# A planned attention-and-experts kernel: deeper buffers, and half of the output blocks turned by DMA instead of TensorE

## The chip, the cores and the metric

The kernel runs on one core of one Trainium2 chip. The metric is device time in microseconds, the median of several runs. The engines are named as the profile names them: PE (TensorE, with PEld for its weight loads), DVE (VectorE), ACT (ScalarE), POOL (GpSimd) and SP (SyncE, which here only issues DMAs). A name with a q behind it (SPq, POOLq) is that engine's instruction sequencer.

## What is computed

The reference is an attention with a learned feature map, followed by a mixture of experts whose routing weights come from eight rounds of row and column scaling. Cut to what matters:

```python
# q, k, v: (8 batches, 8 heads, 576, 64); w_phi: (64, 128)
def phi(x):
    proj = x @ w_phi
    proj = proj - max(abs(proj), axis=-1)
    return concat([exp(proj), exp(-proj)], axis=-1)      # 256 features
q_p, k_p = phi(q), phi(k)
kv = k_p.T @ v;  z = sum(k_p, over the 576 positions)
attn = (q_p @ kv) / (q_p @ z + 1e-6)
x = attn, heads side by side                              # (4608, 512)
P = exp(x @ w_gate - max);  8 times: P /= row sums; P /= column sums; P *= N / E
out = sum over 8 experts e of P[:, e] * (relu(x @ w1[e]) @ w2[e])   # w1: 512x1024
```

## The kernel before

**Tiles.** A batch has 8 heads, taken two at a time: four *pairs* per batch, 32 pairs in all, numbered 0 to 31. A *half* is two pairs and is what one load brings. Of the 576 positions 512 are the main part; the 64 that remain of a batch (the *rest*) are treated for all its heads together. The result x is kept turned, with features on the partitions, in `xT` (four blocks of 128 features by 4608 positions), because every later matmul wants it so.

**Steps.** `pair_a` makes the scores of a pair: matmuls of the turned keys and queries (`qkT`) with `wphi`, the maxima on VectorE (line 459), the exponentials on ScalarE (line 463), and the scaling of v on POOL (line 592). `queries` is its second half. `pair_b` sums keys times values into `kv` and multiplies with the query features (lines 666 and 671); VectorE scales these (lines 678 to 691) into a block `xb`. `pair_c` turns `xb` into `xT`: four TensorE transposes (line 705) into a PSUM bank and one VectorE copy (line 708). `rest_a` and `rest_c` do the same for a batch's rest; the rest's v is scaled by POOL (lines 525 and 529) into `vrd`. `gate` makes a batch's routing logits `L`. `up0` and `down0` are the two layers of expert 0 for one group of 512 positions; they need no routing weights, so they fill TensorE while attention and routing run. Experts 1 to 7 follow with a seven-product matrix scheme (line 1079).

**Loads.** For batches 0 and 1 SP loads q and k in f32 into the accumulators' memory (line 389), and TensorE turns them (line 544). From batch 2 on POOL loads and casts them to bf16 in `qk` (line 395), and a DMA issued by SP turns a half of them into `qkT` (line 412); rests likewise (line 487, `rT`). v comes by SP (line 403). Expert 0's weights come in eight pieces by POOL (lines 371 and 376), those of an expert e from 1 on in two loads of 1 MB (line 361), for expert 1 once `xT` of batch 5 is complete.

**Order.** Nothing is run as written. Each instruction is an `Op` with an estimated duration, the values it reads and writes, and the buffers it takes from a `Ring` of two, three or more. `Plan.schedule` places at each moment the operation that can start first, and by number where several can; the numbers follow the string `order`, one letter for each step (a, q, r, b, c, g, u and d for `up0` and `down0`). What comes out is one fixed row of instructions for each engine, and each engine then works through its row in order. The key `late` marks the point at which the attention's buffers are given back; accumulators 5 to 8 and the later scratch memory `s_p` lie in their place.

Of the kernel before, what the change touches and what calls it, by code (L numbers as in the profile page):

```python
# [9 lines left out]
FP32 = mybir.dt.float32  # L10
# [218 lines left out]
def kernel(  # L229
# [11 lines left out]
    nc = tc.nc  # L241
# [35 lines left out]
    identf = a_in.tile([128, 128], FP32, name="identf")  # L277
    wgate_f = a_in.tile([128, NP, E], FP32, name="wgate_f")
    wphi_f = a_in.tile([128, DF], FP32, name="wphi_f")
# [33 lines left out]

    ring(wp, [128, 4, FF], BF16, "w1", 2)
    ring(wp, [128, 8, DD], BF16, "w2", 2)
    ring(hp, [128, 4, 512], BF16, "hT", 4)
# [3 lines left out]
    ring(a_in, [128, 3 * NP, D], FP32, "v_r", 2)  # L320
    ring(a_t, [128, NP, 128], BF16, "rT", 2)
    ring(a_t, [128, 2, 8, 128], BF16, "qkT", 2)
    ring(a_t, [128, 2, 2, D1], BF16, "kv", 2)
# [3 lines left out]
    ring(a_s, [128, 2, 8], FP32, "m", 2)  # L327
    ring(a_s, [128, 12], FP32, "r", 2)
    ring(a_s, [128, 6], FP32, "rec", 3)
    ring(a_s, [128, NP, 128], BF16, "xb_r", 2)  # L330
    for x in range(2):
        ring(a_t, [128, NP, DF], BF16, f"kr{x}", 2)
        ring(a_t, [128, NP, 128], BF16, f"qr{x}", 2)
        ring(a_t, [128, 8, DF], BF16, f"k{x}", 2)
        ring(a_t, [128, 2, 4, 128], BF16, f"q{x}", 2)
        ring(a_t, [128, 8, D1], BF16, f"v{x}", 2)
        ring(a_s, [128, NP], FP32, f"em_r{x}", 2)
        ring(a_s, [128, 8], FP32, f"em{x}", 2)
    ring("s_p", [128, 1024], BF16, "T", 9)
# [26 lines left out]
    def load_w0(i, r):  # L366

        w1, w2 = W[0]
        n = i % 4
        if i < 4:  # L370
            dma("POOL", 1 << 19, 250, lambda: nc.gpsimd.dma_start(
                out=w1()[:, :, n * 256:(n + 1) * 256],
                in_=moe_w1[0].rearrange("(c p) f -> p c f", p=128)
                [:, :, n * 256:(n + 1) * 256]), r, [(w1, n)])
        else:
            dma("POOL", 1 << 19, 280, lambda: nc.gpsimd.dma_start(
                out=w2()[:, 2 * n:2 * n + 2, :],
                in_=moe_w2[0].rearrange("(c p) f -> p c f", p=128)
                [:, 2 * n:2 * n + 2]), r, [(w2, n)])

    def load_qk(b, hh, nh, t, r=()):

        o = hh % 4
        keys = [o // 2] if nh == 2 else [0, 1]
        if b < 2:
            g = t["f"]
            for x, src in ((1, k), (0, q)):
                i = 2 * x + o // 2
                dma("SP", nh << 17, 320, lambda x=x, src=src, i=i: nc.sync.dma_start(  # L389
                    out=acc[g][:, i:i + nh // 2].rearrange("p a (h c) -> p (a h) c", h=2),  # L390
                    in_=src[b, hh:hh + nh, 0:SM].rearrange("h (p j) d -> p h (j d)", j=NJ)),
                    r, [("acc", g, 2 * x + n) for n in keys])
            return
        for x, src in ((1, k), (0, q)):
            dma("POOL", nh << 17, 230, lambda x=x, src=src: nc.gpsimd.dma_start(
                out=t["qk"]()[:, x, o:o + nh],
                in_=src[b, hh:hh + nh, 0:SM].rearrange("h (p j) d -> p h (j d)", j=NJ)),
                r, [(t["qk"], x, i) for i in keys])

    def load_v(b, hh, nh, t, r=()):  # L400
        o = hh % 4
        keys = [o // 2] if nh == 2 else [0, 1]
        dma("SP", nh << 17, 320, lambda: nc.sync.dma_start(
            out=t["v"]()[:, o:o + nh],
            in_=v[b, hh:hh + nh, 0:SM].rearrange("h (p j) d -> p h (j d)", j=NJ)),
            r, [(t["v"], i) for i in keys])
# [24 lines left out]
    def load_rests(b0, nb, r=()):  # L431
        t = {"v": new("v_r"), "b0": b0}
        if b0 >= 2:
            t["qk"] = new("qk_r")
        for h in range(2):
            rows = slice(h * 64, h * 64 + 64)

            def part(src, h=h):
                return src.rearrange("b (r h) s d -> h s (b r) d", h=2)[
                    h, SM:S, NP * b0:NP * (b0 + nb)]  # L440

            for x, src in ((1, k), (0, q)):
# [6 lines left out]
                dma("POOL", nb << 16, 90, lambda rows=rows, x=x, src=src, part=part:  # L449
                    nc.gpsimd.dma_start(out=t["qk"]()[rows, 0:NP * nb, x, :], in_=part(src)),  # L450
                    r, [(t["qk"], h, x)])
# [17 lines left out]
    def rest_a(b, t):  # L469
# [6 lines left out]
        if b < 2:  # L476
            ptr = new("P1")
            for pr in range(NP):
                pe(128, lambda pr=pr: nc.tensor.transpose(
                    ptr()[:, pr * 128:pr * 128 + 128],  # L480
                    acc[0][:, b, pr * 128:pr * 128 + 128], identf),
                    [("acc", 0, b, h, x) for h in range(2) for x in range(2)] + ["identf"],
                    [ptr, ("acc", 0, b)])
            dve(512, lambda: nc.vector.tensor_copy(
# [35 lines left out]
        for x, s in ((0, -1.0), (1, 1.0)):  # L520
            em = r["em"][x]
            exp(10, lambda em=em: em(), lambda: m()[:, :, 1], s, mk, [em])
            for h in range(2):
                rows = slice(h * 64, h * 64 + 64)
                pool(256, lambda rows=rows, h=h, x=x, em=em: nc.gpsimd.tensor_tensor(
                    out=vrd[b % 2][x][rows, :, h, 0:D], in0=t["v"]()[rows, bi:bi + NP],
                    in1=em()[rows, :, None].to_broadcast([64, NP, D]), op=ALU.mult),
                    [(t["v"], h), em], [("vrd", b % 2, x, h)])
                pool(4, lambda rows=rows, h=h, x=x, em=em: nc.gpsimd.tensor_copy(
                    out=vrd[b % 2][x][rows, :, h, D], in_=em()[rows]),  # L530
# [3 lines left out]
    def pair_a(b, pr, t):  # L534
# [3 lines left out]
        if b < 2:  # L538
            g = t["f"]
            for x in (1, 0):  # L540
                ptr = new("P1")
                i = 2 * x + h0 // 2
                for c in range(4):
                    pe(128, lambda c=c, i=i, ptr=ptr: nc.tensor.transpose(
                        ptr()[:, c * 128:(c + 1) * 128], acc[g][:, i, c * 128:c * 128 + 128],
                        identf), [("acc", g, i), "identf"], [ptr])
                if x:
# [55 lines left out]
        def queries():  # L603

            mq = scores(0, 1)
            for p0 in range(0, 2, 1):
                pt = new("P1")
                for par in range(1):
                    pe(512, lambda par=par, p0=p0, pt=pt: mm(
                        pt()[:, 512 * par:512 * par + 512], wphi2[:, p0 + par, :], qkT(0, 0, 4),  # L610
                        True, True), [(t["T"], 0, h0 // 2), "wphi2"], [pt])
                for y, sg in ((0, 1.0), (1, -1.0)):
# [9 lines left out]
    def pair_b(b, pr, s, r):  # L622
# [29 lines left out]
        def outs(h):  # L652
# [8 lines left out]
            def feats(x):  # L661
# [3 lines left out]
                for j in range(4):  # L665
                    pe(65, lambda j=j: nc.tensor.matmul(  # L666
                        num()[:, j, :], lhsT=s["T"][x]()[:, j % 2, 2 * h + j // 2, :],
                        rhs=kv()[:, x, h, :], start=x == 0 and j == 0, stop=x == 1,
                        skip_group_check=True), keys, [pn])
                if h == 0:  # L670
# [30 lines left out]
    def pair_c(b, pr, xb):  # L701
        if b < 8:
            pxt = new("P1")
# [107 lines left out]
    dma("ACT", 1 << 15, 100, lambda: nc.scalar.dma_start(out=wphi_f[0:64, :], in_=w_phi),  # L811
        w=["wphi_f0"])
    dma("ACT", 1 << 15, 100, lambda: nc.scalar.dma_start(out=wphi_f[64:128, :], in_=w_phi),
        w=["wphi_f1"])
    load_v(0, 0, 2, halves[0, 0])
# [16 lines left out]
    dve(128, lambda: nc.vector.memset(colw, float(E) / float(N)), w=["colw"])  # L832
    dma("SP", 1 << 14, 50, lambda: nc.sync.dma_start(
        out=wgate_f, in_=moe_w_gate.rearrange("(c p) e -> p c e", p=128)), w=["wgate_f"])
    act(32, lambda: nc.scalar.copy(out=wgate, in_=wgate_f), ["wgate_f"], ["wgate"])

    rs, st, qs = {}, {}, {}
# [28 lines left out]
    def stage_g(b):  # L866
# [7 lines left out]
    order = (  # L874
        "raqaqabbccqaqbbaqrbaccuqrbgaqaquabcucbqccaruqbcabqdaqbacbugdqdaqubdccuubauacuqqd"
        "drcbagubqbdaqrduabccauqccubqdcbcuadgqgrbuadqbacaudqbqaddcbaurqcuqbcaadubqauabdqd"
        "gbuccdaqdqbdcbqcuuacbgcqcbcg"
    )
# [406 lines left out]
    for e in range(1, E):  # L1285
        w1, w2 = load_w(e, [("xT", 5, 3)])
        if e == 1:
# [49 lines left out]
```

## Time and profile before

| | |
|---|---|
| median of 3 runs | 1040.92 us (1040.34 to 1041.95) |
| the profiled execution's own time | 1041.77 us |
| its span, first to last instruction | 1040.0 us |
| granted TensorE clock | 0.999 |
| busy share of the span: PE, DVE, ACT, POOL | 98%, 79%, 68%, 44% |
| DMA | 93.94 MB, mean 90 GB/s |

A PE that is busy is not a PE at its peak: matmuls overlap and their ends are modelled, so that only longer idle times show. A DMA share is the mean over 16 engines, and goes over 1 where packets of two queues lie in an engine at the same time.

### The profile page before, as it was taken

The page shows a single profiled execution, that of the slowest core. Times are in us where ns is not written, and L with a number is a line of the kernel's source. Part 1 is how long each engine was busy: PE and PEld are TensorE (multiplying, and loading weights), DVE is VectorE, ACT ScalarE, POOL GpSimd, SP SyncE. Part 2 cuts the span into 40 slices and gives each one's busy share as a digit, 9 for nine tenths or more (in the row PEclk, how much of TensorE's full clock was granted, in tenths as well). Part 3 has the DMA queues.
Part 4 walks back from the last instruction along what each step waited for, and adds up shares of the span by engine and source line. Part 5 has one row for each costly group of instructions (what it writes and reads, how often), then busy time and mean ns, then how long its engine had stood idle before and what let it go on. Part 6 is the DMA issues. An engine that isn't in the chain of part 4 may idle for free.

```text
span 1040.0 us, 24497 instructions
## 1 busy us (share of the span) xinstructions
PE 1014.6 (98%) x9473; PEld 842.0 (81%) x9512; DVE 821.6 (79%) x1626; ACT 711.6 (68%) x1570; POOL 462.2 (44%) x532
## 2 busy tenths in 40 slices
PE   6889999999999999999999999999999999999998
PEld 4556666654788888888888888888888888888886
DVE  6999999988777787778876877788777877787675
ACT  7999999945976666666666665666666656666663
POOL 3886775500234444444434444344444444434442
PEclk9999999999999999999999999999999999999999
DMA  8999979534411161113311441134111611114333
GB/s 240 161 186 144 156 122 173 88 142 112 82 43 51 41 125 50 42 42 83 82 42 42 92 89 45 42 70 99 48 42 48 127 42 42 42 46 128 114 131 122
DMA packets 105237, 93.94 MB, mean 90 GB/s; under 512 B 45344, under 2 KB 80288, under 8 KB 105120
## 3 DMA queue, kind: packets, MB, share of 16 engines
q1 hardware_dynamic: 71840, 68.45, 24.2%
q0 software_dynamic: 33120, 23.86, 16.5%
q8 instruction: 74, 1.21, 0.5%
q14 instruction: 43, 0.35, 0.1%
q10 hardware_dynamic: 160, 0.07, 0.0%
HBM read 94.98 MB, written 14.16 MB: 105 GB/s over the span
## 4 chain that ended last, share of the span: by engine, by line
PE 89%; ACT 3%; DVE 3%; DMA 3%; issue 1%; SPq 0%; DVEq 0%; ACTq 0%
PE P L1079 71%; PE P L467 16%; ACT acc L1241 2%; DMA acc<-in_q_dram 1%; DMA qkT<-qk 1%; PE P L666 1%; DVE m L459 1%; ACT V L1231 1%; PE P L705 1%; ACT U L1107 0%; SPq L389 0%; DVE xb L686 0%; ACT hT L1116 0%; DVE P L678 0%; PE P L671 0%
## 5 line engine op out<-in xcount | busy, mean ns | idle before, releaser
L1234 POOL TENSOR_TENSOR acc<-acc,V 128x512 f32<-128x512 f32 x248 | 317.4, 1287 | 441.0 <-ACT V L1231 437.5
L1111 DVE CUSTOM_DVE_ANT_0 hT<-P,U 128x512 bf16<-128x512 f32 x378 | 255.4, 688 | 129.9 <-ACT U L1107 81.4
L1107 ACT COPY U<-P 128x512 f32<-128x512 f32 x378 | 217.4, 590 | 125.4 <-PE P L1079 120.9
L1231 ACT ACTIVATE V<-P 128x256 f32<-128x256 f32 x496 | 205.8, 476 | 134.7 <-PE P L1079 123.5
L1079 PEld LDWEIGHTS <-w 128*128 128x128 bf16 x2016 | 197.2, 98 | 24.3 <-issue 1.2
L1079 PEld LDWEIGHTS <-S 128*128 128x128 bf16 x1984 | 194.1, 98 | 23.1 <-issue 0.6
L1219 DVE SCALAR_TENSOR_TENSOR acc<-P,acc 128x256 f32<-128x256 f32 x372 | 159.3, 478 | 54.4 <-PE P L1079 51.9
L1079 PEld LDWEIGHTS <-T 128*128 128x128 bf16 x1512 | 147.9, 98 | 18.5 <-issue 1.4
L1079 PEld LDWEIGHTS <-hT 128*128 128x128 bf16 x1488 | 145.4, 98 | 18.2 <-DVE hT L1111 1.1
L1079 PE MATMUL P<-X,w 128*128 128x256 bf16 x1008 | 154.8, 273 | 0.4 <-ACT U L1107 0.4
L1079 PE MATMUL P<-xT,w 128*128 128x256 bf16 x1008 | 151.2, 273 | 0.4 <-ACT acc L794 0.4
L1079 PE MATMUL P<-X,T 128*128 128x256 bf16 x1008 | 148.5, 273 | 0.7 <-ACT U L1107 0.7
L1079 PE MATMUL P<-w,hT 128*128 128x256 bf16 x992 | 142.5, 273 | 0.6 <-DVE hT L1111 0.6
L1079 PE MATMUL P<-T,S 128*128 128x256 bf16 x1056 | 136.3, 273 | 0.4 <-ACT V L1231 0.4
L1079 PE MATMUL P<-w,S 128*128 128x256 bf16 x928 | 126.8, 273 | 0.0
L592 POOL TENSOR_TENSOR v<-v_m,em 128x512 bf16<-128x512 f32 x64 | 66.7, 1042 | 66.1 <-ACT em L463 49.0
L459 DVE TENSOR_REDUCE m<-P 128x4 f32<-128x512 f32 x128 | 83.7, 680 | 4.3 <-PE P L467 2.6
L1116 ACT ACTIVATE hT<-P 128x512 bf16<-128x512 f32 x126 | 73.7, 604 | 12.5 <-PE P L1079 11.9
L987 DVE TENSOR_TENSOR S<-hT 128x1024 bf16<-128x1024 bf16 x124 | 80.2, 683 | 0.0
L467 PE MATMUL P<-w,hT 128*128 128x512 bf16 x301 | 77.6, 379 | 1.2 <-DVE m L459 0.2
L1079 PE MATMUL P<-xT,T 128*128 128x256 bf16 x504 | 75.8, 273 | 0.0
L467 PE MATMUL P<-xT,w 128*128 128x512 bf16 x270 | 73.3, 379 | 1.1 <-DVE m L459 0.2
(94 smaller groups left out, 1088.1 us busy)
## 6 DMA issues: line engine op xcount, KB each, us to landing
X<-xd SPq DMA_DIRECT2D x126, 256.0 KB, 2.6
w<-in_moe_w_dram POOLq DMA_DIRECT2D x14, 1024.0 KB, 10.1
v_m<-in_v_dram SPq DMA_DIRECT2D x15, 512.0 KB, 5.3
out_dram<-acc SPq DMA_DIRECT2D x14, 512.0 KB, 2.9
xd<-S SPq DMA_DIRECT2D x18, 256.0 KB, 2.1
qk<-in_k_dram POOLq DMA_DIRECT2D x12, 256.0 KB, 5.2
qk<-in_q_dram POOLq DMA_DIRECT2D x12, 256.0 KB, 6.2
w<-in_moe_w_dram POOLq DMA_DIRECT2D x8, 256.0 KB, 7.0
```

The source lines that it names most:

```text
L459: dve(el, lambda: nc.vector.tensor_reduce(out=dst(), in_=src(), axis=AX.X, op=ALU.max, apply_absolute_value=True), r, w)
L467: nc.tensor.matmul(out_, lhsT=lhsT, rhs=rhs, start=start, stop=stop)
L592: pool(512, lambda y=y, em=em: nc.gpsimd.tensor_tensor(out=s["v"][y]()[:, :, 0:D], in0=t["v"]()[:, h0:h0 + 2].rearrange("p a (b c) -> p (a ...
L987: lambda: f.tensor_tensor(out=out_(), in0=x(), in1=y(), op=op), r, w, **kw)
L1079: pe(256, lambda i=i, k=k, z=z: nc.tensor.matmul(bank()[:, 256 * i:256 * i + 256], lhsT=lhs(k, i), rhs=rhs(k), start=first and z, stop=k = ...
L1107: act(512, lambda: nc.scalar.copy(out=u[fp][n]().rearrange("p a b -> p (a b)"), in_=x[fp]()), [x[fp]], [u[fp][n]])
L1111: dve(500, lambda: nc.vector._custom_dve(ADD_SAT, out=out_(fp, i, j), in0=bank[fp]().rearrange("p (a b) -> p a b", a=2), in1=u[fp][n](), s ...
L1116: act(512, lambda: nc.scalar.activation(out=out_(fp, i, j), in_=x[fp]().rearrange("p (a b) -> p a b", a=2), func=ACT.Relu, bias=0.0, scale ...
L1219: dve(330, lambda n=n, ts=ts: nc.vector.scalar_tensor_tensor(out=acc[g][:, ts, 256 * j:256 * j + 256], in0=bank()[:, 256 * n:256 * n + 256 ...
L1231: act(390, lambda n=n: nc.scalar.activation(out=u()[:, n, :], in_=bank()[:, 256 * n:256 * n + 256], func=ACT.Copy, bias=0.0, scale=P[:, 4 ...
L1234: pool(670, lambda: nc.gpsimd.tensor_tensor(out=acc[g][:, 2 * i:2 * i + 2, 256 * j:256 * j + 256], in0=acc[g][:, 2 * i:2 * i + 2, 256 * j: ...
L1241: act(512, lambda ts=ts: nc.scalar.activation(out=acc[g][:, ts, :], in_=acc[g][:, ts, :], func=ACT.Copy, bias=0.0, scale=P[:, 4 * g + ts, ...
```

## The change

Seven things are edited, and the string `order` is another one:

- third buffers for `qkT`, `rT`, `kv`, the features, the scaled v and the maxima of a pair, a fourth for `xb`. Room for them comes from the second buffers of `w1` and `w2`, which now lie in `s_p`; so expert 1's weights are loaded after `late`;
- `xb` of batches 3 to 7 (pairs 12 to 31) is turned into `xT` by a DMA that SP issues, without TensorE, PSUM or VectorE;
- the rest's v of batch 0 is scaled by VectorE, that of the other batches by POOL as before;
- the loads of batch 0's second half come in pieces of two heads, keys, queries and values of heads 4 and 5 first;
- half of `w_phi` comes by POOL's queue; `w_gate` is loaded and cast to bf16 by POOL's queue, without the f32 buffer and ScalarE's cast;
- the planner's rates for several loads are lower, and f32 transposes count 260 columns instead of 128;
- some buffers are taken by an earlier operation of their step (the last argument of `pe`).

```diff
-    ring(a_t, [128, 2, 8, 128], BF16, "qkT", 2)
-    ring(a_t, [128, NJ, 128], BF16, "xb", 3)
+    ring(a_t, [128, 2, 8, 128], BF16, "qkT", 3)
+    ring(a_t, [128, NJ, 128], BF16, "xb", 4)
...
-        ring(a_t, [128, 8, DF], BF16, f"k{x}", 2)
+        ring(a_t, [128, 8, DF], BF16, f"k{x}", 3)
...
+        R[tag].make = lambda i, w, tag=tag, shape=shape: (late["s_p"] if i else wp).tile(
+            shape, BF16, name=tag, tag=f"{tag}_{i}")
...
-                dma("SP", nh << 17, 320, lambda x=x, src=src, i=i: nc.sync.dma_start(
+                dma("SP", nh << 17, 268, lambda x=x, src=src, i=i: nc.sync.dma_start(
...
-                pool(256, lambda rows=rows, h=h, x=x, em=em: nc.gpsimd.tensor_tensor(
+                f, eng = (dve, nc.vector) if b == 0 else (pool, nc.gpsimd)
+                f(256, lambda rows=rows, h=h, x=x, em=em, eng=eng: eng.tensor_tensor(
...
-        if b < 8:
+        if b < 3:
             pxt = new("P1")
             for j in range(NJ):
                 pe(128, lambda j=j: nc.tensor.transpose(
...
         else:
             dma("SP", 1 << 17, 148, lambda: nc.sync.dma_start_transpose(
...
-    load_qk(0, 4, 4, halves[0, 1])
-    load_v(0, 4, 4, halves[0, 1])
+    for h0 in (4, 6):
+        load_qk(0, h0, 2, halves[0, 1])
+        load_v(0, h0, 2, halves[0, 1])
+    dma("POOL", 1 << 14, 20, lambda: nc.gpsimd.dma_start(
+        out=wgate, in_=moe_w_gate.rearrange("(c p) e -> p c e", p=128)), w=["wgate"])
...
-        "raqaqabbccqaqbbaqrbaccuqrbgaqaquabcucbqccaruqbcabqdaqbacbugdqdaqubdccuubauacuqqd"
+        "raqaqaqbaqarqbcbabqccbcbraqaubuquacbqbcucgcgacquruabqdbacqabcuadquqaaqqcbcdbdgab"
...
-        w1, w2 = load_w(e, [("xT", 5, 3)])
+        w1, w2 = load_w(e, ["late"])
```

The first place is TensorE's row in the first 20 us. `acc_80` holds q and k of pairs 2 and 3, `acc_79` those of pairs 4 and 5; the matmuls of `vrd` and `v` are pair 0's sums. Before:

```order
54 L544 MATMUL P<-identf,acc_80 128x128 x16
55 L467 LDWEIGHTS kr_234
56 L467 MATMUL P<-vrd_90,kr_234 128x130
57 L544 MATMUL P<-identf,acc_79 128x128 x8
58 L467 LDWEIGHTS kr_239
59 L467 MATMUL P<-vrd_91,kr_239 128x130
60 L467 LDWEIGHTS k_167
61 L467 MATMUL P<-v_206,k_167 128x65
```

And now:

```order
54 L546 MATMUL P<-identf,acc_80 128x128 x16
55 L468 LDWEIGHTS kr_245
56 L468 MATMUL P<-vrd_89,kr_245 128x130
57 L468 LDWEIGHTS kr_251
58 L468 MATMUL P<-vrd_90,kr_251 128x130
59 L468 LDWEIGHTS k_165
60 L468 MATMUL P<-v_203,k_165 128x65
```

The transposes of batch 1's first half have gone from between pair 0's sums to a place behind them.

The second place is SP's row in the middle of the attention, from the loads of batch 4 on. Before, loads of v and turns of q and k alternate:

```order
36 L403 DMA v_m<-in_v_dram 128x4x256
37 L412 DMA_TRANSPOSE qkT<-qk 128x16x128
38 L403 DMA v_m<-in_v_dram 128x4x256
39 L412 DMA_TRANSPOSE qkT<-qk 128x16x128
40 L403 DMA v_m<-in_v_dram 128x4x256
```

And now:

```order
40 L404 DMA v_m<-in_v_dram 128x4x256
41 L714 DMA_TRANSPOSE xT<-xb 128x4x128
42 L413 DMA_TRANSPOSE qkT<-qk 128x16x128
43 L714 DMA_TRANSPOSE xT<-xb 128x4x128
44 L404 DMA v_m<-in_v_dram 128x4x256
45 L453 DMA v_r<-in_v_dram 64x12x64 x2
46 L413 DMA_TRANSPOSE qkT<-qk 128x16x128
```

Turns of finished blocks, which wait for VectorE's `xb`, now stand between the loads and turns that the next pairs need.

The third place is SP's row at the end of the attention. Before:

```order
54 L412 DMA_TRANSPOSE qkT<-qk 128x16x128
55 L403 DMA v_m<-in_v_dram 128x4x256
56 L412 DMA_TRANSPOSE qkT<-qk 128x16x128
57 L403 DMA v_m<-in_v_dram 128x4x256
58 L1063 DMA xd_101<-S 128x1024
```

And now:

```order
64 L714 DMA_TRANSPOSE xT<-xb 128x4x128 x2
65 L413 DMA_TRANSPOSE qkT<-qk 128x16x128
66 L404 DMA v_m<-in_v_dram 128x4x256
67 L714 DMA_TRANSPOSE xT<-xb 128x4x128 x7
68 L1063 DMA xd_100<-S 128x1024
```

The last seven pairs' blocks are turned with no other load behind them but the stores of the experts' sums of x.

More of the change, by code (lines that the diff above doesn't have):

```diff
@@ L277 @@
     identf = a_in.tile([128, 128], FP32, name="identf")
-    wgate_f = a_in.tile([128, NP, E], FP32, name="wgate_f")
     wphi_f = a_in.tile([128, DF], FP32, name="wphi_f")
@@ L312, in ring @@
                       shape, dtype, tag, bufs)
-    ring(wp, [128, 4, FF], BF16, "w1", 2)
-    ring(wp, [128, 8, DD], BF16, "w2", 2)
+    for tag, shape in (("w1", [128, 4, FF]), ("w2", [128, 8, DD])):
+        ring(wp, shape, BF16, tag, 2)
+        R[tag].make = lambda i, w, tag=tag, shape=shape: (late["s_p"] if i else wp).tile(
+            shape, BF16, name=tag, tag=f"{tag}_{i}")
     ring(hp, [128, 4, 512], BF16, "hT", 4)
@@ L370, in load_w0 @@
         if i < 4:
-            dma("POOL", 1 << 19, 250, lambda: nc.gpsimd.dma_start(
+            dma("POOL", 1 << 19, 200, lambda: nc.gpsimd.dma_start(
                 out=w1()[:, :, n * 256:(n + 1) * 256],
@@ L375, in load_w0 @@
         else:
-            dma("POOL", 1 << 19, 280, lambda: nc.gpsimd.dma_start(
+            dma("POOL", 1 << 19, 225, lambda: nc.gpsimd.dma_start(
                 out=w2()[:, 2 * n:2 * n + 2, :],
@@ L394, in load_qk @@
         for x, src in ((1, k), (0, q)):
-            dma("POOL", nh << 17, 230, lambda x=x, src=src: nc.gpsimd.dma_start(
+            dma("POOL", nh << 17, 200, lambda x=x, src=src: nc.gpsimd.dma_start(
                 out=t["qk"]()[:, x, o:o + nh],
@@ L448, in load_rests @@
                     continue
-                dma("POOL", nb << 16, 90, lambda rows=rows, x=x, src=src, part=part:
+                dma("POOL", nb << 16, 100, lambda rows=rows, x=x, src=src, part=part:
                     nc.gpsimd.dma_start(out=t["qk"]()[rows, 0:NP * nb, x, :], in_=part(src)),
@@ L478, in rest_a @@
             for pr in range(NP):
-                pe(128, lambda pr=pr: nc.tensor.transpose(
+                pe(260, lambda pr=pr: nc.tensor.transpose(
                     ptr()[:, pr * 128:pr * 128 + 128],
@@ L482, in rest_a @@
                     [("acc", 0, b, h, x) for h in range(2) for x in range(2)] + ["identf"],
-                    [ptr, ("acc", 0, b)])
+                    [ptr, ("acc", 0, b)], [rT])
             dve(512, lambda: nc.vector.tensor_copy(
@@ L543, in pair_a @@
                 for c in range(4):
-                    pe(128, lambda c=c, i=i, ptr=ptr: nc.tensor.transpose(
+                    pe(260, lambda c=c, i=i, ptr=ptr: nc.tensor.transpose(
                         ptr()[:, c * 128:(c + 1) * 128], acc[g][:, i, c * 128:c * 128 + 128],
-                        identf), [("acc", g, i), "identf"], [ptr])
+                        identf), [("acc", g, i), "identf"], [ptr], [t["T"]])
                 if x:
@@ L610, in queries @@
                         pt()[:, 512 * par:512 * par + 512], wphi2[:, p0 + par, :], qkT(0, 0, 4),
-                        True, True), [(t["T"], 0, h0 // 2), "wphi2"], [pt])
+                        True, True), [(t["T"], 0, h0 // 2), "wphi2"], [pt], own)
                 for y, sg in ((0, 1.0), (1, -1.0)):
@@ L668, in feats @@
                         rhs=kv()[:, x, h, :], start=x == 0 and j == 0, stop=x == 1,
-                        skip_group_check=True), keys, [pn])
+                        skip_group_check=True), keys, [pn], [xb] if x == j == 0 else ())
                 if h == 0:
@@ L810 @@
     load_qk(0, 0, 2, halves[0, 0])
[L811 to L814, printed above, removed]
+    for i, (queue, eng) in enumerate((("ACT", nc.scalar), ("POOL", nc.gpsimd))):
+        dma(queue, 1 << 15, 100, lambda i=i, eng=eng: eng.dma_start(
+            out=wphi_f[64 * i:64 * i + 64, :], in_=w_phi), w=[f"wphi_f{i}"])
     load_v(0, 0, 2, halves[0, 0])
```

25 lines of the change are left out of this document (11 added, 14 removed).

## The prediction

> **What bounds the kernel now.** I read the busy time by stretch first, then the chain that ended last, then the first 22 us in order of time. The columns of the first view are each engine's busy us and count of instructions, the clock and the DMA share.
>
> ```profile
> 20.00:80.00 60.00, 52.73 (x628) 35.69 (x635) 55.82 (x140) 56.63 (x150) 46.24 (x91) 1.00 1.14 175
> 80.00:216.00 136.00, 134.53 (x1535) 89.57 (x1558) 126.54 (x315) 127.12 (x325) 81.31 (x162) 1.00 0.81 129
> 216.00:254.00 38.00, 37.75 (x197) 18.35 (x198) 33.33 (x90) 14.10 (x25) 0.82 (x1) 1.00 0.43 149
> 254.00:295.00 41.00, 38.33 (x309) 29.92 (x309) 30.20 (x52) 40.64 (x79) 9.82 (x9) 1.00 0.43 88
> 295.00:1028.00 733.00, 733.00 (x6717) 657.00 (x6716) 558.91 (x1001) 460.17 (x960) 315.09 (x250) 1.00 0.26 68
> ```
>
> From 80 us on PE (first column) is idle for 1.5 us in 136, then 0.25 in 38; in the experts not at all. Only before 80 us does it lose much: 7.3 us in 20 to 80, with VectorE and ScalarE at 93 and 94%. The chain, in order of time, says the same:
>
> ```profile
> 60.42 14.05 DMA qkT<-qk
> 74.52 0.84 PE P L467 x6
> ...
> 214.69 0.22 PE P L705 x4
> 214.91 1.48 PE P L467 x35
> ...
> 216.47 10.15 PE P L467 x49
> ...
> 253.75 0.47 DVE P L946
> 254.25 3.17 ACT acc L1241 x5
> ...
> 294.82 733.76 PE P L1079 x6720
> ```
>
> After a DMA that turns q and k lands at 74.5, PE carries the chain until the routing weights exist (line 946), ScalarE carries it for 40 us, and PE the rest. So a microsecond of TensorE work removed between 75 and 254 us is a microsecond of time, as long as nothing else runs dry. Experts 1 to 7 (733.76 us) are not edited, so the sum concerns the first 295 us.
>
> **The transposes that go.** Line 705 runs 128 times; batches 3 to 7 hold 5 x 4 pairs x 4 = 80 of these. The chain has four in 0.22 us, 0.055 each: 80 x 0.055 = 4.4 us. They all stand after pair 11, in the stretch where PE has no idle time to swallow the saving: **-4.4**. With them go 20 VectorE copies of line 708, some 8 us of VectorE's time; PE, not VectorE, sets the pace there, so I count nothing for them.
>
> **The start.**
>
> ```profile
> 14.11 0.34 ACT L463 ACTIVATE em_r<-m_r 128x4 f32<-128x4 f32 x2
> 16.93 0.61 POOL L525 TENSOR_TENSOR vrd<-v_r,em_r 64x256 bf16<-64x256 f32 x1
> 17.06 0.22 PE L467 MATMUL P<-vrd,kr 128*128 128x130 bf16 x1
> 17.48 0.22 ACT L835 CAST wgate<-wgate_f 128x32 bf16<-128x32 f32 x1 [2.06 <-DMA wgate_f<-in_moe_w_gate_dram]
> 18.92 1.04 POOL L592 TENSOR_TENSOR v<-v_m,em 128x512 bf16<-128x512 f32 x1 [1.22 <-issue]
> 19.29 1.06 PE L544 MATMUL P<-identf,acc 128*128 128x128 f32 x8 [2.01 <-DMA acc<-in_k_dram]
> 20.19 0.22 PE L467 MATMUL P<-vrd,kr 128*128 128x130 bf16 x1
> 20.25 0.68 PE L467 MATMUL P<-v,k 128*128 128x65 bf16 x16
> 15.00:20.00 5.00, 2.27 (x20) 2.10 (x21) 1.43 (x4) 2.94 (x9) 3.58 (x10) 1.00 1.00 265
> ```
>
> Pair 0's sums begin at 17.06 and go on at 20.19, because the transposes of batch 1 stand between them and wait 2.01 us for their load. That wait leaves this place, as the order shows; ScalarE's wait of 2.06 us for `w_gate` goes too. What is late next: the sums want the rest's v, now scaled by VectorE. The eight instructions, four of them 64x256, cost VectorE between 4 x 0.28 us (its 128x128 product, below) and 4 x 0.61 (POOL's own time for the same): 1 to 2.5 us. VectorE is busy 1.43 of the 5 us from 15 to 20, so they fit. The gain lies between nothing (a later load stops PE instead; the DMA share is 1.00 here) and 20.19 - 17.06 = 3.1 us. I take the middle: **-1.5**.
>
> ```profile
> L691 DVE TENSOR_TENSOR xb_r<-P,rec 128x128 bf16<-128x128 f32 x32 | 8.9, 280 | 0.0
> L987 DVE TENSOR_TENSOR S<-hT x124: 673/683/723, 269.1 to 1017.8; 128x1024 bf16<-128x1024 bf16 x124
> ```
>
> VectorE products with two SBUF inputs show no long ones beside a busy POOL: 673 to 723 ns over 124 of them (minimum, median, maximum). The Trainium skill, page "SBUF — State Buffer", section "Who interferes with whom", says that such a product contends with GpSimd instructions that read SBUF, and that the loser blocks for the whole instruction. By that rule each of the four could stand behind one POOL product of 1.04 us, 4.2 us in all, and the start would gain nothing. The trace does not show it, though the planner keeps line 987 and POOL apart (`shared=True`) and doesn't keep these apart, so it isn't disproved.
>
> **The turns by DMA.** Nothing in the trace turns `xb` by DMA, but SP turns the rests' q and k, 128 KB as well, and halves of 512 KB (duration of the issue, then time to landing, minimum, median and maximum):
>
> ```profile
> L412 SPq DMA_TRANSPOSE qkT<-qk x12: 1317/3248/7542, 43.6 to 180.8; - x12
> DMA to landing us min/median/max: 4.3/7.5/14.0
> L487 SPq DMA_TRANSPOSE rT<-qk_r x6: 1190/1222/1488, 53.9 to 138.9; - x6
> DMA to landing us min/median/max: 4.6/6.5/6.9
> ```
>
> In the middle this latency is covered: in the new order each group's first expert matmul on `xT` of batches 3 to 7 has over 13 us of other PE work between it and the end of that batch's pairs (matmuls counted, at 0.03 to 0.21 us each). At the end it isn't. The last gate needs pair 31's block; between pair 31's last output matmul and that gate PE has 19 expert matmuls at 10.15 / 49 = 0.207, four transposes (0.22) and one gate's 16 short ones (0.4): 4.6 us.
>
> ```profile
> 213.04 0.12 PE P L666 x4
> ...
> 213.84 0.42 DVE L686 TENSOR_TENSOR xb<-P,rec 128x256 bf16<-128x256 f32 x1
> ...
> DMA  9999999939999950000000000000000000000199
> ```
>
> `xb` is complete 1.1 us after the last output matmul (214.26 - 213.16). With a landing of 4.3 to 6.9 us the gate waits 0.8 to 3.4 us; below nothing is excluded, since a wait can't gain. I take the low end, because the DMA engines stand idle then (the last line is their busy tenths from 180 to 220 us): **+0.8**. Everything behind the gate (routing, then ScalarE's rescaling) moves by the same.
>
> **Third buffers and the new order.** Counted in PE's row, when 112 of expert 0's matmuls are done, 13 pairs had their outputs before, 15 now; at 160, 16.5 and 18.5. So the attention runs two pairs further ahead of PE's filler, which third buffers permit, and VectorE must deliver that.
>
> ```profile
> L459 DVE TENSOR_REDUCE m<-P 128x4 f32<-128x512 f32 x84 | 55.1, 681 | 2.4 <-ACT k L463 1.2 <-PE P L467 0.9
> ```
>
> From 80 to 216 us, 84 reductions at four a pair are 21 pairs, in 126.54 us of VectorE: 6.0 each. Two pairs are 12 us of VectorE, while PE has their own 6.7 us of work more in hand: 5.3 us must come out of idle time that VectorE had. It had 4.2 us in 20 to 80 and more in the first 20. If it finds none, PE waits 5.3; if the buffers let it run without gaps, nothing. I take **+1.0**.
>
> **At nothing:** expert 1's weights, at 10.1 us a load (below), land some 20 us after the attention; PE wants them 40 us after it. If that cover went, PE would stand for the difference. `w_phi` and `w_gate` on POOL's queue: POOL idles until 9.6 us.
>
> ```profile
> w<-in_moe_w_dram POOLq DMA_DIRECT2D x14, 1024.0 KB, 10.1
> ```
>
> **The sum.** -4.4 - 1.5 + 0.8 + 1.0 = -4.1 on the profiled span of 1040.0: 1035.9. That execution took 1041.77, 1.77 more than its span, and lay 0.85 above the median; so the runs should have 1040.92 - 4.1 = **1036.8**. Its own range, with the start between nothing and -3.1 and the order between nothing and +3, is 1034 to 1040. What a measurement here tells from no change is about 0.2%, 2.1 us: 1038.8 to 1043.0 counts as the same.
>
> **Rivals.**
>
> *More comes of the buffers* (0.13). VectorE's and ScalarE's idle 6 to 7% before 80 us is where two buffers stop them; half of PE's 7.3 us returns, and the whole 3.1 of the start: -4.4 - 3.1 - 3.6 = -11.1, 1029.8. Against it: the chain there goes over a DMA.
>
> *VectorE becomes the bound* (0.22). The full 5.3 is paid: -4.4 - 1.5 + 0.8 + 5.3 = +0.2, 1041.1. For it: 93% busy in both stretches. Against: 8 us less work for it.
>
> *The last turn is slow* (0.05): 3.4 instead of 0.8 at the gate, 1039.4.
>
> *The DMA queue becomes the bound* (0.12), and the kernel slower. In 20 to 80 the DMA share is 1.14. One turn of q and k took 14.05 us instead of the median 7.5, landed at 74.47, and PE used it at 74.52. If that happens to two halves, because turns of `xb` hold SP or the engines, PE stands twice for 6.5 us: -4.1 + 13.1, 1049.9. It decides from the point at which a half lands after its pair's turn on PE; before, that slack was nil at 74.5. Against it: the third `qkT` lets a half be turned earlier, and counted in PE's row over 16 us of its work lie between the last `xb` turn ahead of a half on SP and the first use of that half. The skill's page "VectorE: DVE Perf Modes", section "The three transpose paths", speaks for this rival: it gives 1309 ns for one 128x128 block by DMA against 390 on TensorE, and advises TensorE where PSUM will do. Taken block by block, 80 blocks would be 105 us of turning, an estimate from that page, and the attention would be bound by it. The trace disagrees as to throughput: sixteen blocks land within 4.3 us.
>
> **How the numbers follow.** The forecast has 0.48. Faster by over 0.2%: most of the forecast, the first rival and a little of the third, 0.60; same: most of the second, the rest of the forecast and of the third, 0.22; slower: the fourth and the second's upper part, 0.18. The range reaches down to 1031, into the first rival, and up to 1044; the fourth rival and the end of the first are left out, about 2 in 10.
>
> **What would show it.** Right: no line 705 beyond 48 instructions; PE's idle time from 80 us to the routing still near 1%; pair 0's sums together near 17 us; the experts' 733.76 us unchanged, about 4 us earlier. Wrong: PE waiting for `qkT` turns, for line 459 or 678, or several us at the last gate; or a ScalarE stretch before the experts that is longer than 40 us.

## The result: 0.33% faster, about what was forecast

The changed kernel took 1037.58 us (median of 7 runs, 1036.82 to 1039.34) against 1040.92 us (7 runs): a ratio of 0.9967, 95% interval 0.9955 to 0.9978, or 3.4 us less. The forecast was 1036.8, 4.1 us less. The total held. Of its four terms the transposes held, the start came out worse than forecast, and the order and the last gate came out better.

The profiled execution has a span of 1036.3 us, 3.7 less than before. First the busy time by stretch, in the columns of the prediction (PE, PEld, DVE, ACT, POOL, clock, DMA share); the first row is that of the kernel before for the first 20 us, the others are those of the changed kernel:

```profile
0.00:20.00 20.00, 10.86 (x69) 8.04 (x70) 12.19 (x24) 12.88 (x34) 7.28 (x21) 1.00 0.91 248
```
```profile
0.00:20.00 20.00, 11.13 (x62) 7.57 (x63) 14.56 (x29) 14.13 (x36) 8.43 (x19) 0.99 0.91 238
20.00:80.00 60.00, 54.23 (x642) 37.89 (x647) 57.05 (x144) 55.21 (x147) 43.17 (x85) 0.97 1.23 180
80.00:216.00 136.00, 132.95 (x1471) 86.08 (x1495) 122.38 (x304) 126.16 (x325) 83.09 (x164) 1.00 0.87 134
216.00:254.00 38.00, 37.79 (x183) 18.16 (x186) 33.53 (x86) 17.62 (x30) 0.75 (x1) 1.00 0.75 196
254.00:295.00 41.00, 38.95 (x327) 31.63 (x326) 28.61 (x50) 39.73 (x78) 11.00 (x9) 1.00 0.40 89
295.00:1028.00 733.00, 732.95 (x6702) 655.68 (x6702) 560.64 (x1003) 458.39 (x956) 315.62 (x250) 1.00 0.27 68
```

PE's idle time (length of the stretch less PE's busy time) fell by 0.3 us in the first 20 us, by 1.5 from 20 to 80, and by 0.6 from 254 to 295; from 80 to 216 it rose from 1.5 to 3.05. Nothing moved from 216 to 254 or in the experts. The new item is the clock, 0.97 in the second row and 1.00 before. It comes from one place:

```profile
18.00:20.00 2.00, 0.23 (x1) 0.11 (x2) 1.96 (x5) 1.53 (x4) 2.00 (x5) 0.91 1.17 322
20.00:24.00 4.00, 3.88 (x38) 3.57 (x38) 3.32 (x7) 1.57 (x4) 0.03 (x1) 0.62 1.41 194
```

PE stands almost idle from 18 to 20 us and is then granted 0.62 in the mean of four microseconds. If its 3.88 us of work there are all stretched by the slow clock, that is 3.88 x 0.38 = 1.5 us more of work (an estimate). The rows then add up: -4.4 for the transposes, -0.3, -1.5, +1.6 and -0.6 of idle time, +1.5 of clock: -3.7, which is the span's difference. That it fits to the tenth is chance: the profile's page has PE's busy time only 2.5 us lower (1014.6 and 1012.1) where these terms say 2.9. And stretched work need not cost time, since it can fill time in which PE would have waited. The experiments on the start come back to this.

In the chain of waits a turn of q and k still ends at 74.5 us, and the last expert's closing matmuls begin at 1025.24 us; the last fence is their row in the kernel before, 1028.63. In order of time (second fence) the last step of the routing weights starts at 249.88, where it started at 253.75. So the gain, 3.9 us by then, is made before the routing ends. By the closing matmuls it is 3.4 us, so the lower idle time from 254 to 295 us was no gain in time:

```profile
58.31 16.11 DMA qkT<-qk
74.47 0.41 PE P L468 x2
...
1025.24 6.87 PE P L468 x31
```
```profile
249.88 0.45 DVE L946 TENSOR_TENSOR P<-T,c_bc 128x288 f32<-128x288 f32 x1
```
```profile
1028.63 6.87 PE P L467 x31
```

### The profile page after: what moved, and what is told of

Read it like the earlier page. It is cut to its first block, busy times and chain, and to the rows that moved or that the text cites. A ratio compares the mean times of both kernels' runs of the same rounds, so it can differ in the third digit from the quotient of the medians.

```text
span 1036.3 us, 24359 instructions
## 1 busy us (share of the span) xinstructions
PE 1012.1 (98%) x9396; PEld 838.7 (81%) x9432; DVE 819.0 (79%) x1614; ACT 711.2 (69%) x1569; POOL 462.1 (45%) x526
## 4 chain that ended last, share of the span: by engine, by line
PE 90%; DVE 3%; ACT 2%; DMA 2%; issue 1%; POOL 0%; DVEq 0%; ACTq 0%; POOLq 0%
PE P L1079 73%; PE P L468 16%; DMA qkT<-qk 2%; PE P L668 1%; DVE m L460 1%; ACT acc L1241 1%; ACT U L1107 0%; DVE xb L688 0%; DVE P L680 0%; PE P L673 0%; ACT k L464 0%; PE P L546 0%; ACT q L464 0%; ACT V L1231 0%; DVE xb_r L693 0%
## 5 line engine op out<-in xcount | busy, mean ns | idle before, releaser
L1079 PEld LDWEIGHTS <-T 128*128 128x128 bf16 x1512 | 147.9, 98 | 19.5 <-issue 2.3
L464 ACT ACTIVATE k<-P 128x512 bf16<-128x512 f32 x128 | 69.0, 629 | 5.7 <-PE P L468 4.6
```

Source lines behind the costliest of these rows:

```text
L464: act(el, lambda: nc.scalar.activation(out=dst(), in_=src(), func=ACT.Exp, bias=0.0, scale=scale), r, w)
L1079: pe(256, lambda i=i, k=k, z=z: nc.tensor.matmul(bank()[:, 256 * i:256 * i + 256], lhsT=lhs(k, i), rhs=rhs(k), start=first and z, stop=k = ...
```

## The experiments

Each was timed in turns with the kernel before, on one chip; ratios are to the kernel before, with 95% intervals. Two experiments are compared by their ratios, so a difference of less than some 0.002 between them (an estimate from the intervals) is not sure. Where it is changed who turns a block, the planner lays all rows anew, and the time holds that too. The changed kernel's own is 0.9967, and 0.001 is 1.04 us.

### What the DMA turns are worth: all blocks on TensorE

```diff
-        if b < 3:
+        if b < 8:
             pxt = new("P1")
```

> The changed kernel with all 32 blocks turned by TensorE and copied by VectorE. Theory A (the 80 transposes are worth their 4.4 us and the DMA turns cost nothing): 1041.5 to 1042.5. Rival B (the DMA turns cost waits of their own): less than 3.5 us slower, 1038 to 1041. Rival C (the 20 copies also weigh on a full VectorE): 1043 or more.

1.0011 (1.0001 to 1.0021): 4.6 us slower than the changed kernel, 3 to 6 by the two intervals. Theory A fits best, though the interval just reaches C. The 80 transposes were costed at 4.4, and in the changed order their replacement by DMA costs nothing that shows. Everything else in the change, taken together, brings nothing: with TensorE's turns it stands 1.1 us above the kernel before.

### The DMA turns alone, in the kernel before

```diff
-        if b < 8:
+        if b < 3:
             pxt = new("P1")
```

> The kernel before with nothing but the turns of batches 3 to 7 by DMA: two buffers, the old order string, the old loads. Theory A (the gain is that of the transposes alone; buffers, order and start cancel): -4.4 and up to 0.8 back at the last gate, 1036.5 to 1037.5. Rival B (with three xb and two of the rest, the turns hold the buffers longer and stall the pairs, so the third buffers are what makes the turns pay): 1039 to 1042.

1.0055 (1.0040 to 1.0070): 5.7 us slower than the kernel before, although PE has 4.4 us less to do. Rival B's sign, and more than its size. Between 110 and 216 us PE was idle for 1.15 us before (first row) and is idle for 6.36 here (second):

```profile
110.00:216.00 106.00, 104.85 (x1206) 70.04 (x1224) 99.10 (x250) 99.27 (x256) 64.20 (x130) 1.00 0.78 124
```
```profile
110.00:216.00 106.00, 99.64 (x1079) 63.70 (x1096) 90.12 (x221) 97.50 (x253) 64.68 (x131) 1.00 0.93 148
```

In the view of waits (us in all, times, the longest) and in the chain there is a wait that the kernel before does not have: PE for a turn, once 2.1 us long (in the middle, at the first place of the second fence) and once 0.6 (at the last gate).

```profile
PE P L467 <- DMA xT<-xb: 2.7, 2, 2.1
```
```profile
120.81 6.76 DMA xT<-xb
...
219.72 2.46 DMA xT<-xb
```

So the latency that is hidden in the changed kernel is not hidden everywhere. These 2.7 us are about half of the 5.2 us of idle time that came in from 110 to 216; the rest is not attributed.

### Which part hides it: the order or the buffers

Old order string in the changed kernel:

```diff
-        "raqaqaqbaqarqbcbabqccbcbraqaubuquacbqbcucgcgacquruabqdbacqabcuadquqaaqqcbcdbdgab"
+        "raqaqabbccqaqbbaqrbaccuqrbgaqaquabcucbqccaruqbcabqdaqbacbugdqdaqubdccuubauacuqqd"
...
```

> The changed kernel with the order string of the kernel before; third buffers, DMA turns, loads and start as changed. Theory A (third buffers are what the DMA turns need; the new order matters little): a ratio to the kernel before of 0.995 to 0.998, near the changed kernel's 0.9967. Rival B (the new order is what hides the turns; with the old one the waits of the run that had DMA turns alone, 1.0055, come back): 1.002 to 1.006.

1.0105 (1.0089 to 1.0120). Rival B, beyond its range. The same with all blocks on TensorE (`if b < 8`):

> The changed kernel with the old order string and all blocks turned by TensorE: third buffers, loads and start as changed. Against the run with the old order string and DMA turns (1.0105) and against the kernel before. Theory A (the DMA turns cause the loss under the old order): 0.997 to 1.001, so the turns cost some 10 us there. Rival B (the old string does not fit the changed loads, rates and buffers, whoever turns the blocks): 1.008 to 1.014.

1.0078 (1.0066 to 1.0090), between the theories and nearer to B: most of the loss is of the old string under the changed loads, rates and buffers. The turns add 2.8 us to it where 4.4 should have been saved, 7 us of waits by inference from the times. And the new order with the old buffers, for `qkT` as shown and for `rT`, `kv`, `xb`, `m`, `r`, `k`, `q`, `v` and `em` likewise:

```diff
-    ring(a_t, [128, 2, 8, 128], BF16, "qkT", 3)
+    ring(a_t, [128, 2, 8, 128], BF16, "qkT", 2)
...
```

> The changed kernel with all buffers of the pairs as before (two, and three xb), the new order string and the turns of batches 3 to 7 by DMA. The planner lays its rows anew. Theory A (the new order alone hides the turns, as little came of third buffers under the old order): 0.996 to 1.000. Rival B (order and buffers belong together: the new order runs pairs ahead that two buffers cannot hold): 1.003 to 1.012.

1.0124 (1.0111 to 1.0138), rival B, just over the end of its range: this order needs these buffers. In these three the planner lays all rows anew, so they tell that order and buffers belong together, and not what each is worth.

### One batch more by DMA

```diff
-        if b < 3:
+        if b < 2:
```

> The changed kernel with batch 2's four blocks turned by DMA as well. Theory A (each PE transpose is worth 0.055 us, and VectorE, full from 80 to 110 us, is spared four copies of 0.33 us): 0.9 to 2.2 us faster than the changed kernel, ratio 0.9945 to 0.996. Rival B (here the turns stand among the loads and the turns of q and k, with DMA shares over 1, and make a half late): 1 to 5 us slower, ratio 0.998 to 1.001.

1.0041 (1.0029 to 1.0054), 7.7 us slower than the changed kernel: rival B, and more. SP's row in order of time (start, duration), first of the changed kernel, then of this one:

```profile
99.09 1.20 SPq L714 DMA_TRANSPOSE xT<-xb  x1
100.45 5.41 SPq L413 DMA_TRANSPOSE qkT<-qk  x1
```
```profile
93.04 14.09 SPq L714 DMA_TRANSPOSE xT<-xb  x3
107.26 0.50 SPq L404 DMA_DIRECT2D v_m<-in_v_dram  x1
108.35 5.93 SPq L413 DMA_TRANSPOSE qkT<-qk  x1
```

And the chain of this kernel at that place:

```profile
93.04 9.64 DMA xT<-xb
...
108.35 12.07 DMA qkT<-qk
```

Three turns of finished blocks hold SP for 14.09 us, since the last of them waits for its block; the turn of q and k behind it goes out 8 us later than in the changed kernel (108.35 instead of 100.45). By the chain, a gate matmul of PE waits for the first of the three turns (9.64 us from issue to landing), and that makes the next block late, which holds SP, which makes the half late (12.07 us). PE stood 2.0 us for the turned block and 1.8 us for the half. This is the mechanism of the prediction's fourth rival, one step beyond the change, with the gate's wait besides.

### The start: where batch 0's scaling runs

In the changed kernel, first the scaling instructions of batch 0 in order of time (what ended an idle time is in brackets):

```profile
16.80 0.42 DVE L527 TENSOR_TENSOR vrd<-v_r,em_r 64x256 bf16<-64x256 f32 x1
17.00 1.14 POOL L594 TENSOR_TENSOR v<-v_m,em 128x512 bf16<-128x512 f32 x1 [0.35 <-ACT em L464]
17.15 1.02 DVE L531 CAST vrd<-em_r 64x4 bf16<-64x4 f32 x1
18.22 0.23 PE L468 MATMUL P<-vrd,kr 128*128 128x130 bf16 x1 [0.41 <-DVE vrd L531]
18.24 1.28 POOL L594 TENSOR_TENSOR v<-v_m,em 128x512 bf16<-128x512 f32 x1
18.54 1.01 DVE L531 CAST vrd<-em_r 64x4 bf16<-64x4 f32 x1
19.90 0.17 DVE L531 CAST vrd<-em_r 64x4 bf16<-64x4 f32 x1
20.12 0.27 PE L468 MATMUL P<-vrd,kr 128*128 128x130 bf16 x1 [1.67 <-DVE vrd L531]
```

The products take 0.42 us, but two copies of four elements take 1.02 and 1.01 instead of 0.17. Each starts after a POOL product and ends with it (17.00 + 1.14 and 17.15 + 1.02; 18.24 + 1.28 and 18.54 + 1.01). Pair 0's sums, forecast together near 17 us, come at 18.22 and 20.12. Three places for this work were tried, in the same rows otherwise:

```diff
-                f(4, lambda rows=rows, h=h, x=x, em=em, eng=eng: eng.tensor_copy(
+                f(4, lambda rows=rows, h=h, x=x, em=em: nc.gpsimd.tensor_copy(
```

> The changed kernel with the four one-column copies of batch 0's rest (line 531) on POOL; the four products (line 527) stay on VectorE, all else in the same places. Theory A: two of these copies took 1.02 and 1.01 us instead of 0.17 because POOL's product of v (line 594) ran beside them; that made PE wait 1.67 us, and the granted clock fell to 0.50 behind it. Without them pair 0's sums run together at about 18.3 to 18.6 us, the clock stays at 1.00 from 20 to 24 us, and the time falls by 1.5 to 3 us against the changed kernel: 1034.5 to 1036. Rival B: VectorE, full from 30 to 110 us, swallows what the start gains: the first 25 us improve and the time stays at 1037 to 1038.

0.9948 (0.9931 to 0.9964), 2.0 us less than the changed kernel, which these intervals don't make sure. It is A's size, but not its place:

```profile
17.52 1.21 POOL L594 TENSOR_TENSOR v<-v_m,em 128x512 bf16<-128x512 f32 x1
17.83 1.18 DVE L527 TENSOR_TENSOR vrd<-v_r,em_r 64x256 bf16<-64x256 f32 x1
19.38 0.22 PE L468 MATMUL P<-vrd,kr 128*128 128x130 bf16 x1 [1.64 <-POOL vrd L531]
```
```profile
20.00:24.00 4.00, 3.55 (x35) 2.57 (x31) 3.97 (x8) 3.27 (x9) 1.39 (x4) 1.00 1.37 203
```

Now a product (1.18 instead of 0.42) waits for POOL's to end, and the second sum comes at 19.38. The clock stays at 1.00 in the profiled execution (the row by stretch, in the second fence). That is not shown to be where the gain comes from. The mean clock of the six executions was 1.000 twice and 0.997 or 0.998 four times, as low as in the changed kernel; the two took 1037.10 and 1038.46 us, the four 1034.71 to 1040.36. Products and copies both on POOL, as before the change:

```diff
-                f, eng = (dve, nc.vector) if b == 0 else (pool, nc.gpsimd)
+                f, eng = (dve if b == 0 else pool, nc.gpsimd)
```

> The changed kernel with the products and the copies of batch 0's rest both on POOL, as before the change, in the same places of the row. Theory A (the copies on VectorE lost what the products gained): POOL has some 3.4 us of them ahead of pair 0's v, so the sums come at 20 to 21 us, as in the changed kernel, and the time is 1037 to 1038.5. Rival B (the step to VectorE gained 1.5 us, as predicted): 1039 or more.

0.9966 (0.9954 to 0.9978), theory A: nothing was gained by the step to VectorE. The second sum comes at 20.64, and the clock is at 0.50 from 20 to 24 us (order of time, and the row by stretch). That is lower than the changed kernel's 0.62, at the same ratio:

```profile
20.64 0.27 PE L468 MATMUL P<-vrd,kr 128*128 128x130 bf16 x1 [2.43 <-POOL vrd L531]
```
```profile
20.00:24.00 4.00, 3.36 (x31) 3.04 (x31) 1.53 (x3) 1.05 (x3) 2.04 (x6) 0.50 1.44 178
```

Last, the copies on ScalarE:

```diff
-                f(4, lambda rows=rows, h=h, x=x, em=em, eng=eng: eng.tensor_copy(
+                g = nc.scalar.copy if b == 0 else nc.gpsimd.tensor_copy
+                f(4, lambda rows=rows, h=h, x=x, em=em, g=g: g(
```

> The changed kernel with the four one-column copies of batch 0's rest on ScalarE, where no product of POOL's can hold them; the four products stay on VectorE. Theory A (VectorE's work of two SBUF inputs or of SBUF copies and POOL's product of v hold each other up until the first of them ends): at most one product still stands behind POOL's, the second sum of vrd starts at 18.6 to 19.2 us instead of 20.12, the clock stays at 1.00, and the ratio to the kernel before falls from 0.9967 to 0.9940 to 0.9955. Rival B (VectorE and ScalarE, full from 30 to 110 us, swallow it, and ScalarE has 0.8 us more): 0.996 to 0.997.

0.9945 (0.9933 to 0.9957), 1036.25 us beside 1041.89 for the kernel before: 2.3 us faster than the changed kernel (the intervals overlap by 0.0002), and the lowest ratio of all, though not clearly below that with the copies on POOL (0.9948). The second sum starts at 17.95, earlier than A said:

```profile
17.47 1.32 POOL L595 TENSOR_TENSOR v<-v_m,em 128x512 bf16<-128x512 f32 x1
17.95 0.23 PE L468 MATMUL P<-vrd,kr 128*128 128x130 bf16 x1 [1.40 <-DVE vrd L527]
```
```profile
20.00:24.00 4.00, 3.55 (x47) 2.62 (x45) 3.97 (x9) 4.00 (x12) 1.74 (x3) 1.00 1.15 315
```
```profile
L527 DVE TENSOR_TENSOR vrd<-v_r,em_r x4: 417/424/1244, 15.3 to 17.5; 64x256 bf16<-64x256 f32 x4
```

One product still stands behind POOL's (the longest of the four, 1244 ns, in the last fence), and one of POOL's has 1.32 us. Over the four versions the time falls with the start of the second sum: 20.64 and 20.12 (0.9966, 0.9967), 19.38 (0.9948), 17.95 (0.9945).

### From 80 to 110 us: is VectorE or ScalarE the bound?

PE lost 0.3 us here before and loses 2.0 now, while both other engines are full (before, changed). The 1.6 and 5 us that the first text below gives for this stretch are not in these rows:

```profile
80.00:110.00 30.00, 29.68 (x330) 19.52 (x334) 27.44 (x66) 27.86 (x70) 17.11 (x33) 1.00 0.91 144
```
```profile
80.00:110.00 30.00, 28.02 (x330) 18.92 (x334) 29.66 (x74) 29.79 (x78) 24.08 (x43) 1.00 1.07 158
```

The changed kernel's chain goes over VectorE for 13.8 of these 30 us, above all from 97 to 107, and most often over its maxima, as here; before the change it went over PE alone:

```profile
99.06 1.61 DVE m L460 x3
...
104.44 1.79 DVE m L460 x3
```

In the first run VectorE, in the second ScalarE too has less to do in this stretch:

```diff
                       lambda pp=pp: pp().rearrange("p (a b) -> p a b", a=4 * n)
+                      [:, :, 0:32 if 10 <= NP * b + pr < 17 else 128],
```

> The changed kernel in which the maxima of pairs 10 to 16 are taken over 32 of each 128 values, so that VectorE does these 28 reductions in about 0.3 instead of 0.68 us (part of the maxima is left out). Same places in each row. Theory A (between 80 and 110 us VectorE, idle for 0.3 us, sets the pace, and PE loses there some 5 us against 1.6 before the change): PE's lost time from 80 to 110 falls to 2 or 3 us and the kernel is 2 to 3 us faster, ratio 0.994 to 0.995. Rival B (ScalarE, as full there, or the turns by DMA set the pace): within 0.7 us of the changed kernel, ratio 0.996 to 0.9975.

```diff
+                        if y == 1 and 10 <= NP * b + pr < 17:
+                            act(512 * n, lambda y=y, c0=c0, pp=pp: nc.vector.tensor_copy(
+                                out=s["E"][y]()[:, 2 * c0:2 * c0 + 4 * n].rearrange(
+                                    "p a b -> p (a b)"), in_=pp()), [pp], [(s["E"][y], c0)])
+                            continue
```

> The kernel of the run with part of the maxima, in which in addition the second exponential of the keys of pairs 10 to 16 (14 instructions of some 0.6 us on ScalarE) is a plain copy of the same shape on VectorE, which has 8 us to spare there (these exponentials are left out, so the features of those pairs are not the reference's). Same places in each row. Theory A (between 80 and 110 us ScalarE, busy 29.8 of 30 us and never waiting, sets the pace): PE's lost time there falls by 1.5 to 3 us against the run with part of the maxima, ratio to the kernel before 0.993 to 0.9945 against 0.9958. Rival B (neither engine: the turns and loads of q and k do): within 0.7 us of that run, 0.995 to 0.9965.

0.9958 (0.9946 to 0.9971) and 0.9968 (0.9955 to 0.9980): neither time differs clearly from the changed kernel's.

```profile
80.00:110.00 30.00, 28.01 (x326) 19.16 (x331) 21.50 (x72) 29.95 (x81) 24.41 (x46) 1.00 1.06 156
```
```profile
80.00:110.00 30.00, 28.78 (x342) 19.13 (x340) 28.69 (x87) 25.40 (x67) 22.95 (x42) 1.00 1.27 181
```

VectorE with 8.5 us to spare leaves PE exactly as it was (28.01), so VectorE alone, though 99% busy and on the chain, does not set the pace. ScalarE with 4.6 us to spare gives PE 0.8 us at most (this profile holds 36 more matmul records than the others, so part of it is only recorded), and the time does not follow. Neither full engine by itself sets the pace. That the two together do is not excluded: with VectorE relieved ScalarE was busy for 29.95 us, and in the second run the copies brought VectorE back to 28.69. In the changed kernel's view of waits PE's gaps here are 0.2 to 0.5 us long, 0.8 us in all behind VectorE and 0.5 behind POOL; what sets the pace stays open.

### One batch less by DMA, on the fastest version

```diff
-        if b < 3:
+        if b < 4:
```

> The kernel with the four one-column copies on ScalarE (0.9945 of the kernel before), in which batch 3's four blocks are turned by TensorE again, so that the DMA turns begin with batch 4, behind the stretch in which loads and turns of q and k share the queue. Theory A (where the order was written for them, the turns of batch 3 cost nothing): 16 transposes more, +0.9 us and perhaps 1 us for the planner's new rows, ratio 0.9950 to 0.9965. Rival B (the turns of batch 3 delay turns of q and k, and are part of what PE loses between 80 and 150 us): 1 us or more faster, ratio under 0.9938.

0.9965 (0.9952 to 0.9979) against 0.9945: 2.1 us slower, theory A at its upper end, though the intervals overlap a little. So batch 3's turns probably pay too, and three is the best of the thresholds tried (two on the changed kernel, four on its fastest version), each with the planner's own rows.

## Why the prediction was right, point by point

- **The transposes (-4.4): right.** Turning the blocks on TensorE again cost 4.6 us. The 48 that are left take the place foreseen. They belong to 12 of the 32 blocks, so five eighths of the blocks go by DMA, more than the half of the title.
- **The start (-1.5): the step that failed.** It had pair 0's sums together near 17 us; they came at 18.22 and 20.12, the second as late as before (20.19). It said that the eight instructions on VectorE fit in 1 to 2.5 us, and that the trace shows no long ones beside POOL. Their work fits; their waits were left out, because line 987, on which that rested, is kept apart from POOL by the planner. PE's idle time of the first 20 us fell by 0.3, and the low clock stretched its work by up to 1.5: between -0.3 and +1.2 instead of -1.5. The Trainium skill's rule (page "SBUF — State Buffer", section "Who interferes with whom") would have made it nothing. Here the traces agree with that rule for the products: VectorE's of two SBUF inputs (1.18, 1.24 instead of 0.42) end 0.3 us after POOL's, and POOL's is longer (1.28, 1.32 instead of the 1.04 it had before the change) where a VectorE product started within 0.04 us of it. VectorE's copies (1.02, 1.01), which have one input, end with POOL's product. With the copies on ScalarE, a step that the prediction did not have, the time fell by 2.3 us.
- **Third buffers and the new order (+1.0): within its range, and the mechanism only half.** PE's idle time fell by 1.5 from 20 to 80 us and rose by 1.6 behind it: +0.1. From 80 us to the routing it is 1.9% of the time, where the prediction's sign was near 1%. VectorE was named as what would be short; it was full, and time given to it alone brought nothing. What the term missed is that the order and the buffers are the condition for the -4.4: under the old order the turns cost 7 us of waits with third buffers, and 10 with two (the latter with the old loads too), by inference from the times.
- **The last gate (+0.8): came out as nothing.** In the changed kernel pair 31's block is complete at 208.91 and PE reaches the gate at 212.13:

```profile
208.48 0.43 DVE L688 TENSOR_TENSOR xb<-P,rec 128x256 bf16<-128x256 f32 x1
212.13 0.54 PE L468 MATMUL P<-wgate,xT 128*128 128x8 bf16 x16
```
```profile
L714 SPq DMA_TRANSPOSE xT<-xb x20: 1189/1199/2143, 99.1 to 208.9; - x20
DMA to landing us min/median/max: 2.4/3.8/9.1
```

  The landing was taken from turns in more traffic: the 4.3 us are the least of a 512 KB half, the 128 KB turns of the rests took 4.6 at least. The last three turns, from 200 us on, landed in 2.4, 2.5 and 4.0 us, and PE came to the last gate 3.2 us after the block was complete without waiting. Where PE stands directly at the gate, as in the kernel before with DMA turns, the wait is there, 0.6 us.
- **ScalarE's stretch:** 0.6 us less idle time from 254 to 295, which no step had; it was no gain in time, since from the last step of the routing weights to the closing matmuls the changed kernel takes 775.4 us instead of 774.9.
- **The sum:** the start was 1.2 to 2.7 us too favourable; 0.9 from the order and 0.8 from the gate came the other way. The total was right partly by luck, because these errors cancel.
- **The rivals:** the DMA queue as bound (0.12) is what comes one batch further on; in the changed kernel a half did turn in 16.11 us, and PE waited for it for 0.8. VectorE as bound (0.22) looks true in the busy share and in the chain from 80 to 110 us, but the 5.3 us were not paid, and time given to VectorE alone brought nothing. Of what the first rival wanted back from 20 to 80 us (3.6), 1.5 came.

## What to carry to other kernels

A transpose moved from a busy TensorE to a DMA is worth its matmul time only if its latency has cover and its queue has nothing urgent behind it: test it together with the buffers and the order that give the cover, since each alone can be a loss. An engine that is 99% busy isn't for that the bound: take work from it and see whether the waiting engine moves. A low clock in a profile isn't for that lost time: see whether executions without it are faster. When small work goes to VectorE, look at what POOL does in the same microsecond, since the shortest instruction can wait for the longest.

## What the hardware showed that was not expected

- A VectorE copy of 64x4 elements took 1.02 us beside a POOL product, 0.17 alone; a 64x256 product 1.24, 0.42 alone.
- PE's granted clock fell to 0.50 for some 3.4 us in the changed kernel, from about 19.7 to 23.1 us (rows of the first fence). It fell during the wait of 1.67 us, 1.2 us after PE's last matmul had ended (18.22 + 0.23), with 0.23 us of work from 18 to 20 us. In the kernel before, a wait of 2.01 us with 0.71 us of work in the same 2 us (second fence) left it at 1.00, and so did the wait of 1.64 us with the copies on POOL. What level of activity decides, these traces do not tell. The Trainium skill's page "TensorE: Matmul & The Clock Gate", section "What's actually happening", puts the fall behind at least one idle window of about 3.4 us; in this trace PE was not wholly idle ahead of it: from 16.0 to 19.5 us it was busy for 1.5 us, most of it with f32 transposes.

```profile
19.50:20.00 0.50, 0.00 (x0) 0.00 (x0) 0.49 (x3) 0.03 (x1) 0.50 (x3) 0.66 1.36 243
20.00:23.00 3.00, 2.88 (x26) 2.62 (x26) 2.47 (x5) 0.57 (x2) 0.03 (x1) 0.50 1.48 189
23.00:23.50 0.50, 0.50 (x10) 0.48 (x9) 0.43 (x1) 0.50 (x3) 0.00 (x0) 0.93 1.18 217
```
```profile
18.00:20.00 2.00, 0.71 (x7) 0.74 (x8) 0.04 (x1) 2.00 (x7) 1.08 (x2) 1.00 0.87 169
```

- A turn of 128 KB from SBUF to SBUF landed in 2.4 to 9.1 us: 6.6 in the median from 95 to 125 us, where the DMA share is 1.31, and 2.5 from 200 us on, where it is 0.17 to 212. It held SP for 1.2 us in the median; three turns, of which the last waited for its block, held it for 14.09.
